# Moving one head's output weights onto eight DMA engines in small pieces, and splitting the result's transfer, in a decode kernel bound by its DMA stream

## The chip, the cores and the metric

One core of a Trainium2 chip. The metric is device microseconds of one execution. A "span" is what the profile covers, from the first to the last recorded instruction; it is about 1.8 us shorter than the time of the same execution (357.64 us and 355.8 us for the profiled execution of the kernel before).

## The reference

A decode step of one token through a conditioned transformer block, everything in bfloat16. It streams 149.4 MB, nearly all of it the key and value caches (8 heads of 32768 x 128, for each of K and V).

```python
def reference(A_x, A_k_cache, A_v_cache, A_wq, A_wo, B_x, B_w1, B_w2, c, w_mod):
    def _A_ref(x, k_cache, v_cache, wq, wo):          # 32 query heads, 8 kv heads, Dh = 128
        q = (x @ wq).reshape(B, Sq, Hq, Dh).transpose(0, 2, 1, 3)
        k, v = repeat(k_cache, 4), repeat(v_cache, 4)
        p = softmax(einsum('bhqd,bhkd->bhqk', q, k) * Dh ** -0.5)
        o = einsum('bhqk,bhkd->bhqd', p, v)
        return o.transpose(0, 2, 1, 3).reshape(B, Sq, Hq * Dh) @ wo      # wo is 4096 x 512
    def _B_ref(x, w1, w2):
        return maximum(x @ w1, 0) @ w2                                   # 512 -> 1792 -> 512
    sa, ca, ga, sb, cb, gb = split(silu(c) @ w_mod, 6)
    x = x + ga * _A_ref(layernorm(x) * (1 + ca) + sa, ...)
    return x + gb * _B_ref(layernorm(x) * (1 + cb) + sb, ...)
```

## The kernel before

Everything large comes through one ring of four slots of 32 KB a partition. All loads are issued on the sync engine's queue in one fixed order; a load goes out when the slot that it reuses is free.

```python
    WOP = [(0, Hkv // 2), (Hkv // 2, Hkv // 4), (3 * Hkv // 4, Hkv // 4)]   # wo in three parts, by kv heads
    ring = ctx.enter_context(tc.tile_pool(name="ring", bufs=4))
    ...
    def load(key):
        ...
        elif kind == "wo":
            t = ring.tile([P, WOP[key[1]][1] * REP, D], BF16, tag="slot", name="wo_sb")
            src = wo_v(key[1])
        ...
        stream_dma(t[:], src)                         # nc.sync.dma_start

    stream = [("wm",), ("wq",)] + [("k", 0, (2 * G, 2 * G + 1)) for G in range(NG)]
    for g in range(LAST):
        for G in range(NG):
            stream += [(kind, gg, (2 * G, 2 * G + 1)) for kind, gg in (("k", g + 1), ("v", g))]
    stream += [("v", LAST, (0, 1)), ("v", LAST, (2,)), ("wo", 0), ("wo", 1), ("v", LAST, (3,)), ("wo", 2)]
    stream += [("w1",)] + [("w2", i) for i in range(len(W2P))]
```

So the output weights of heads 0 to 5 are loaded near the end, and their products with the attention output run while the PE waits for the last piece of V (2.8 us of that wait are left in the profile). The tail after that piece is short: the product with the last part of wo, a layer norm, w1, w2, two vector operations and the result's transfer.

```python
                if g == LAST and u == NTILE - 1:
                    for i in range(len(WOP) - 1):
                        project(i)                    # 96 small matmuls, before the last V piece is used
                pv(g, u)
    ...
    project(len(WOP) - 1)
    ...
    nc.vector.tensor_tensor(out=o_bf[:], in0=o_rows[:], in1=x1_rows[:], op=ALU.add)
    nc.scalar.dma_start(
        out=out[0, 0].rearrange("(i n) -> i n", i=KT),
        in_=o_bf[:].rearrange("(i r) n -> i r n", r=32)[:, 0, :],
    )
```

## Time and profile before

| kernel before | us |
|---|---|
| first three runs, median (lowest to highest) | 357.16 (357.08 to 357.24) |
| with the fourth, profiled run | 357.2 (357.08 to 357.69) |
| the profiled execution, time and span | 357.64, 355.8 |

How to read it: the DMA engines are full from start to end (share 1.00 at 432 GB/s from 10 to 318 us, 0.58 in the last stretch, 347 to 352 us; in the packet records 16 packets are in flight at each of 17 moments from 10 to 330 us), so the time is bytes over rate plus the ragged end, at which the 16 engines do not finish together. The first fence is from the page of the kernel before (destination, source, issuing engine, count, KB each, us from issue to landing):

```profile
wo_sb<-in_A_wo_dram SPq DMA_DIRECT2D x1, 2048.0 KB
wo_sb<-in_A_wo_dram SPq DMA_DIRECT2D x2, 1024.0 KB, 10.2
```

The output weights, 4 MB, are three transfers, each over 128 partitions. The second is from the instructions in order of time (start us, duration us, engine, line, operation, and in brackets how long the engine had been idle and what ended that):

```profile
330.82 0.33 SPq L118 DMA_DIRECT2D Vsb<-in_A_v_cache_dram  x1
334.06 3.34 PE L461 MATMUL attnT_ps<-o_sb,wo_sb 128*128 128x1 bf16 x96
...
349.56 1.02 PE L525 MATMUL ffn_ps<-w_sb,hidT 128*1 128x128 bf16 x32 [0.98 <-DMA w_sb<-in_B_w_dram]
350.85 0.60 PE L525 MATMUL ffn_ps<-w_sb,hidT 128*1 128x128 bf16 x16 [0.26 <-DMA w_sb<-in_B_w_dram]
351.94 0.38 PE L525 MATMUL ffn_ps<-w_sb,hidT 128*1 128x128 bf16 x8 [0.50 <-DMA w_sb<-in_B_w_dram]
```

The last eight matmuls start at 351.94 us, after 0.50 us of idleness that a DMA of w2 ended. That start is the best single number for "when did the stream end".

### The profile page before, as it was taken

Reading aid. Unit: us, or ns where it says so; the run is one execution under the profiler, and the core shown is the slowest. Engines: PE = TensorE matmul, PEld = TensorE weight load, DVE = VectorE, ACT = ScalarE, POOL = GpSimd, SP = SyncE. Lnnn points to the kernel's source line nnn. Section 1 sums busy time; section 2 is a strip of 40 time slices with the busy share of each in tenths; the row PEclk is TensorE's granted clock in tenths of the full one; section 3 lists DMA queues with packets and bytes.
Section 4 is the critical chain, followed back from the end, with each engine's and each line's share of the span. In section 5 each row is a group of like instructions: output and inputs, shape, how many; then the busy total and the mean of one; then the engine's idle time right before and its main releaser. Section 6 shows DMA issues by size and latency. Waiting matters only on the chain.

```text
span 355.8 us, 4200 instructions
## 1 busy us (share of the span) xinstructions
PE 274.2 (77%) x1859; PEld 129.9 (37%) x1859; DVE 188.0 (53%) x210; ACT 30.8 (9%) x74; POOL 8.5 (2%) x14
## 2 busy tenths in 40 slices
PE   0552875998689885998499849987799859987754
PEld 0540322343333342443244324433243324335753
DVE  8414696783297409661759157642937184832020
ACT  1022002201200120001100120012000110003000
POOL 9000000000000000000000000000000000000000
PEclk9999968799969996999699978998599969997555
DMA  8999999999999999999999999999999999999993
GB/s 321 442 422 440 431 427 442 429 425 438 435 426 438 431 422 446 427 431 440 424 442 435 422 443 427 431 437 427 431 437 428 427 438 433 424 437 424 408 411 130
DMA packets 6604, 149.69 MB, mean 421 GB/s; under 512 B 697, under 2 KB 698, under 8 KB 1594
## 3 DMA queue, kind: packets, MB, share of 16 engines
q1 hardware_dynamic: 6578, 149.43, 97.9%
q8 instruction: 14, 0.23, 0.2%
q14 instruction: 4, 0.03, 0.0%
q10 hardware_dynamic: 8, 0.00, 0.0%
HBM read 149.42 MB, written 0.00 MB: 420 GB/s over the span
## 4 chain that ended last, share of the span: by engine, by line
DMA 47%; PE 34%; DVE 14%; issue 3%; ACT 0%; SPq 0%; DVEq 0%
DMA Ksb<-in_A_k_cache_dram 42%; PE S_ps L343 18%; PE o_ps L412 12%; DVE KTt L334 11%; DMA Vsb<-in_A_v_cache_dram 3%; DMA w_sb<-in_B_w_dram 2%; PE oT_ps L402 1%; DVE PT_g L381 1%; PE oT_ps L429 1%; DVE S_g L349 1%; PE L_ps L386 0%; SPq L118 0%; PE attnT_ps L461 0%; PE mT_ps L359 0%; ACT X L426 0%
## 5 line engine op out<-in xcount | busy, mean ns | idle before, releaser
L343 PE MATMUL S_ps<-KTt,qbd 128*128 128x512 bf16 x512 | 134.5, 423 | 29.8 <-DVE KTt L334 29.7
L334 DVE STREAM_TRANSPOSE KTt<-Ksb 128x2048 f32<-128x2048 f32 x64 | 142.6, 2279 | 21.1 <-DMA Ksb<-in_A_k_cache_dram 17.0
L412 PE MATMUL o_ps<-Vsb,PT_g 128*16 128x512 bf16 x448 | 99.0, 379 | 0.0
L343 PEld LDWEIGHTS <-qbd 128*128 128x128 bf16 x512 | 53.8, 106 | 104.6 <-issue 53.8
L412 PEld LDWEIGHTS <-PT_g 128*16 128x16 bf16 x448 | 39.1, 90 | 56.8 <-issue 3.0
L436 DVE TENSOR_TENSOR oT_sb<-oT_ps,Linv 128x4 bf16<-128x4 f32 x8 | 1.3, 162 | 71.8 <-PE oT_ps L429 57.3
L349 DVE TENSOR_SCALAR_CACHE_REDUCE S_g<-S_ps 128x512 f32<-128x512 f32 x16 | 11.1, 691 | 41.3 <-PE S_ps L343 41.3
L314 ACT COPY qbd<-qrep_sb 32x128 bf16<-32x128 bf16 x32 | 9.4, 295 | 160.0 <-PE S_ps L343 158.9
L386 PE MATMUL L_ps<-Lexp,ones_f 128*128 128x4 f32 x16 | 3.9, 314 | 13.0 <-DVE Lexp L384 13.0
L426 ACT COPY X<-o_ps 16x512 f32<-16x512 f32 x7 | 4.0, 574 | 110.4 <-PE o_ps L412 110.4
L402 PE MATMUL oT_ps<-PT_g,Vsb 128*128 128x4 bf16 x256 | 7.3, 166 | 4.4 <-DMA Vsb<-in_A_v_cache_dram 2.8
L381 DVE STREAM_TRANSPOSE PT_g<-P_g 128x1024 bf16<-128x1024 bf16 x8 | 9.9, 1232 | 0.0
L429 PE MATMUL oT_ps<-osel,X 16*128 16x4 f32 x56 | 7.3, 250 | 2.5 <-ACT nbias L373 2.5
L197 PE MATMUL xc_ps<-one,c_bd 8*128 8x1 bf16 x4 | 0.3, 172 | 11.6 <-DVE c_bd L187 11.6
L376 ACT ACTIVATE P_g<-S_g,nbias 128x1024 bf16<-128x1024 f32 x8 | 9.2, 1147 | 0.2
L402 PEld LDWEIGHTS <-Vsb 128*128 128x128 bf16 x256 | 7.2, 105 | 4.5 <-DMA Vsb<-in_A_v_cache_dram 2.9
L359 PE MATMUL mT_ps<-ident_f,m_p 128*1 128x128 f32 x8 | 2.2, 269 | 8.4 <-DVE m_p L357 8.4
L386 PEld LDWEIGHTS L_ps<-Lexp,ones_f 128*128 128x128 f32 x16 | 3.6, 271 | 13.5 <-issue 13.4
L155 DVE COPY sel<-ident_bf 128x128 bf16<-128x128 bf16 x4 | 7.8, 3823 | 0.4 <-POOL ident_bf masks.py:199 0.4
L429 PEld LDWEIGHTS oT_ps<-osel,X 16*128 16x128 f32 x56 | 6.7, 186 | 3.1 <-ACT nbias L373 3.1
L292 PE MATMUL qT_ps<-hT,wq_sb 128*128 128x1 bf16 x128 | 3.6, 165 | 3.2 <-DMA wq_sb<-in_A_wq_dram 3.2
L359 PEld LDWEIGHTS mT_ps<-ident_f,m_p 128*1 128x1 f32 x8 | 0.6, 80 | 12.2 <-issue 9.2
(94 smaller groups left out, 79.4 us busy)
## 6 DMA issues: line engine op xcount, KB each, us to landing
Ksb<-in_A_k_cache_dram SPq DMA_DIRECT2D x16, 4096.0 KB, 29.7
Vsb<-in_A_v_cache_dram SPq DMA_DIRECT2D x15, 4096.0 KB, 25.5
wq_sb<-in_A_wq_dram SPq DMA_DIRECT2D x1, 4096.0 KB, 19.7
Vsb<-in_A_v_cache_dram SPq DMA_DIRECT2D x2, 2048.0 KB, 15.5
wm_sb<-in_w_mod_dram SPq DMA_DIRECT2D x1, 3072.0 KB, 10.2
wo_sb<-in_A_wo_dram SPq DMA_DIRECT2D x1, 2048.0 KB
wo_sb<-in_A_wo_dram SPq DMA_DIRECT2D x2, 1024.0 KB, 10.2
w_sb<-in_B_w_dram SPq DMA_DIRECT2D x1, 1792.0 KB, 10.5
```

What stands on the lines that cost most here:

```text
L155: nc.vector.tensor_copy(out=sel[:, hp, :].rearrange("p (a c) -> p a c", a=4), in_=src)
L314: nc.scalar.copy(out=o, in_=i)
L334: nc.vector.transpose(out=KTt[:].bitcast(F32), in_=Ksb[:, 32 * half:32 * half + 32, :].rearrange("p j d -> p (j d)").bitcast(F32),)
L343: nc.tensor.matmul(S_ps[:], lhsT=qbd[g % 2][:, hp, s, :], rhs=KTv[:, 16 * sl:16 * sl + 16, h, :, par], start=(t4 == 0 and sl == 0 and hp = ...
L349: nc.vector.tensor_scalar(out=S_tiles[g][:, G, :], in0=S_ps[:], scalar1=1.0, scalar2=None, op0=ALU.mult, op1=ALU.max, accum_out=m_tiles[g] ...
L376: nc.scalar.activation(out=P_g[:], in_=S_g[:].rearrange("p g f -> p (g f)"), func=ACT.Exp, bias=nbias[:], scale=scale, accum_out=l_g[:],)
L381: nc.vector.transpose(out=PT_g[:], in_=P_g[:])
L386: nc.tensor.matmul(L_ps[:], lhsT=ones_f[:], rhs=Lexp[:], start=True, stop=True)
L402: nc.tensor.matmul(o_tiles[g][:], lhsT=Vsb[:, j, :], rhs=PT_g[:, c0:c0 + REP], start=(u == 0 and j == 0), stop=(u == NTILE - 1 and j == TK ...
L412: nc.tensor.matmul(o_tiles[g][:], lhsT=PT_g[:, c0:c0 + 16], rhs=Vsb.rearrange("p (s j) d -> p s j d", j=16)[:, :, j, :], start=(u == 0 and ...
L426: nc.scalar.copy(out=X[:], in_=oT_ps[:])
L429: nc.tensor.matmul(oT_ps[:], lhsT=X[:, s * Dh:(s + 1) * Dh], rhs=osel[:, s, :], start=(s == 0), stop=(s == 3),)
```

## The change

The weights of head 0 get a tile of their own on partitions 0 to 63. They are brought in by eight transfers of eight partitions each (64 KB), one after each K or V load in the turns of heads 1 and 2, in the first half of the stream. The weights of heads 1, 2 and 3 come in two transfers into one ring slot, ahead of the loads of head 4's turn, and heads 0 to 3 are projected in the middle of the stream instead of at the end. The weights of heads 4 to 7 stay late. The result leaves in two transfers of two rows, on the sync and the scalar queue. One buffer each of two smaller tiles was given up to make room. The intent, as I read it: to give eight of the sixteen DMA engines a little more and the other eight a little less, so that all end together, to take work from the end, and to save issuing time at the result.

```diff
-    WOP = [(0, Hkv // 2), (Hkv // 2, Hkv // 4), (3 * Hkv // 4, Hkv // 4)]
+    WOP = [(0, 1, P // 2), (1, 1, P), (2, 2, P), (4, 2, P), (6, 2, P)]      # third: partitions
...
+        if kind == "wo_lo":
+            lo = 32 * (key[1] // 4) + key[1] % 4
+            stream_dma(wo_lo[lo:lo + 29:4], wo_v(0)[lo:lo + 29:4])
+            loaded[key] = True
+            if key[1] == 7:
+                loaded[("wo", 0)] = wo_lo[:]
+            return
...
+        elif kind == "wo12":
+            n1, n2 = wo_rows(1), wo_rows(2)
+            t = ring.tile([P, n1 + n2, D], BF16, tag="slot", name="wo_sb")
+            loaded[("wo", 1)], loaded[("wo", 2)] = t[:, 0:n1, :], t[:, n1:n1 + n2, :]
+            stream_dma(loaded[("wo", 1)], wo_v(1))
+            stream_dma(loaded[("wo", 2)], wo_v(2))
+            return
...
     for g in range(LAST):
+        if g == Hkv // 2:
+            stream.append(("wo12",))
         for G in range(NG):
-            stream += [(kind, gg, (2 * G, 2 * G + 1)) for kind, gg in (("k", g + 1), ("v", g))]
-    stream += [("v", LAST, (0, 1)), ("v", LAST, (2,)), ("wo", 0), ("wo", 1), ("v", LAST, (3,)), ("wo", 2)]
+            for kind, gg in (("k", g + 1), ("v", g)):
+                stream.append((kind, gg, (2 * G, 2 * G + 1)))
+                if 1 <= g < 3:
+                    stream.append(("wo_lo", 4 * (g - 1) + 2 * G + (kind == "v")))
+    stream += [("v", LAST, (0, 1)), ("v", LAST, (2,)), ("wo", 3), ("v", LAST, (3,)), ("wo", 4)]
...
+    wo_lo = const.tile([P // 2, wo_rows(0), D], BF16)
...
-        PT_g = spool.tile([P, NG * 512], BF16, tag="PT_g", name="PT_g", bufs=3)
+        PT_g = spool.tile([P, NG * 512], BF16, tag="PT_g", name="PT_g")
...
-            X = spool.tile([16, 4 * Dh], F32, tag="X", name="X")
+            X = spool.tile([16, 4 * Dh], F32, tag="X", name="X", bufs=1)
...
     for g in range(Hkv):
+        if g == Hkv // 2:
+            for i in range(3):
+                project(i)
...
-                    for i in range(len(WOP) - 1):
-                        project(i)
+                    project(3)
...
-    nc.scalar.dma_start(out=out[0, 0].rearrange("(i n) -> i n", i=KT), in_=...)
+    o_v = o_bf[:].rearrange("(i r) n -> i r n", r=32)[:, 0, :]
+    out_v = out[0, 0].rearrange("(i n) -> i n", i=NROW)
+    nc.sync.dma_start(out=out_v[0:2], in_=o_v[0:2])
+    nc.scalar.dma_start(out=out_v[2:4], in_=o_v[2:4])
```

More of the change, by code (lines that the diff above doesn't have):

```diff
@@ L45 @@
     NG = NTILE // 2
-    WOP = [(0, Hkv // 2), (Hkv // 2, Hkv // 4), (3 * Hkv // 4, Hkv // 4)]
+    WOP = [(0, 1, P // 2), (1, 1, P), (2, 2, P), (4, 2, P), (6, 2, P)]
     LAST = Hkv - 1
+    NROW = 4
+    RW = D // NROW
     FB = 2
@@ L63, in wo_v, with wo_rows @@
     def wo_v(i):
-        g0, n = WOP[i]
-        return A_wo[g0 * REP * Dh:(g0 + n) * REP * Dh, :].rearrange("(p r) d -> p r d", p=P)
+        g0, n, pp = WOP[i]
+        return A_wo[g0 * REP * Dh:(g0 + n) * REP * Dh, :].rearrange("(p r) d -> p r d", p=pp)
+    def wo_rows(i):
+        return WOP[i][1] * REP * Dh // WOP[i][2]
     w1_v = B_w1.rearrange("(p kt) f -> p kt f", p=P)
@@ L100, in load @@
         elif kind == "wo":
-            t = ring.tile([P, WOP[key[1]][1] * REP, D], BF16, tag="slot", name="wo_sb")
+            t = ring.tile([P, wo_rows(key[1]), D], BF16, tag="slot", name="wo_sb")
             src = wo_v(key[1])
+        elif kind == "wo12":
[5 more added lines that the diff above has]
+            return
         elif kind == "w1":
@@ L165 @@
     cmask, rsel = {}, {}
-    for n in sorted({n * REP for _, n in WOP}):
+    for n in sorted({wo_rows(i) for i in range(len(WOP))}):
         cmask[n] = const.tile([P, P // n], F32, name=f"cmask{n}")
@@ L180 @@
     oT_sb = const.tile([P, Hq], BF16)
-    oA = [const.tile([P, n * REP, P // (n * REP)], BF16, name=f"oA{i}") for i, (_, n) in enumerate(WOP)]
+    oA = [const.tile([P, n * REP, P // wo_rows(i)], BF16, name=f"oA{i}") for i, (_, n, _) in enumerate(WOP)]
     one8 = const.tile([8, 1], BF16)
@@ L255, with to_rows @@
     nc.vector.tensor_copy(out=modT_sb[:], in_=modT_ps[:])
-    def rows4(src_T, r_ps, name):
-        for i in range(KT):
+    def to_rows(src_T, r_ps, name):
+        for i in range(NROW):
             dst = r_ps[32 * i:32 * i + 1, :].rearrange("o (n kt) -> o kt n", kt=KT)
@@ L262, in rows4 @@
                 m = nc.tensor.matmul(
-                    dst[:, kt, :], lhsT=src_T[:, kt:kt + 1], rhs=ident_f[:, 32 * i:32 * i + 32],
+                    dst[:, kt, :], lhsT=src_T[:, kt:kt + 1], rhs=ident_f[:, RW // KT * i:RW // KT * (i + 1)],
                     start=True, stop=True, skip_group_check=True,
@@ L266, in rows4 @@
                 tc.stamp_issue_order_token(m.ins, "pe_tail")
-        r_sb = const.tile([P, P], F32, name=f"{name}_sb")
+        r_sb = const.tile([32 * NROW, RW], F32, name=f"{name}_sb")
         nc.scalar.copy(out=r_sb[:], in_=r_ps)
         return r_sb
-    gb_ps = ps_s.tile([P, 512], F32, tag="s", name="gb_ps")[:, 0:P]
+    gb_ps = ps_s.tile([P, 512], F32, tag="s", name="gb_ps")[0:32 * NROW, 0:RW]
     nc.vector.memset(gb_ps, 0.0)
-    gb_rows = rows4(modT_sb[:, 5 * KT:6 * KT], gb_ps, "gb_rows")
+    gb_rows = to_rows(modT_sb[:, 5 * KT:6 * KT], gb_ps, "gb_rows")
     hT = const.tile([P, KT], BF16)
@@ L418, in part_of @@
     def part_of(g):
-        return [i for i, (g0, n) in enumerate(WOP) if g0 <= g < g0 + n][0]
+        return [i for i, (g0, n, _) in enumerate(WOP) if g0 <= g < g0 + n][0]
     def normalise(g):
@@ L432, in normalise @@
         i = part_of(g)
-        g0, n = WOP[i]
-        CH = P // (n * REP)
+        g0 = WOP[i][0]
+        RH = wo_rows(i)
+        CH = Dh // RH
         o_g = oT_sb[:, REP * g:REP * (g + 1)]
@@ L439, in normalise @@
             in0=o_g.unsqueeze(2).to_broadcast([P, REP, CH]),
-            in1=cmask[n * REP][:].unsqueeze(1).to_broadcast([P, REP, CH]), op=ALU.mult,
+            in1=cmask[RH][:].unsqueeze(1).to_broadcast([P, REP, CH]), op=ALU.mult,
         )
@@ L445, in spread @@
     def spread(i):
-        n = WOP[i][1] * REP
-        o2_ps = small_ps([P, n], "o2_ps")
+        pp, RH = WOP[i][2], wo_rows(i)
+        o2_ps = small_ps([pp, RH], "o2_ps")
         nc.tensor.matmul(
-            o2_ps[:], lhsT=oA[i][:].rearrange("p h c -> p (h c)"), rhs=rsel[n][:], start=True, stop=True,
+            o2_ps[:], lhsT=oA[i][:].rearrange("p h c -> p (h c)"), rhs=rsel[RH][:], start=True, stop=True,
         )
-        o2 = const.tile([P, n], BF16, name=f"o2_sb{i}")
+        o2 = const.tile([pp, RH], BF16, name=f"o2_sb{i}")
         nc.vector.tensor_copy(out=o2[:], in_=o2_ps[:])
@@ L456, in project @@
     def project(i):
-        n = WOP[i][1] * REP
         wo_sb = need(("wo", i))
-        for r in range(n):
+        for r in range(wo_rows(i)):
             for ko in range(KT):
@@ L463, in project @@
                     lhsT=wo_sb[:, r, :].rearrange("p (m ko) -> p ko m", ko=KT)[:, ko, :],
-                    rhs=o2_tiles[i][:, r:r + 1], start=False, stop=(i == len(WOP) - 1 and r == n - 1),
-                    skip_group_check=True,
+                    rhs=o2_tiles[i][:, r:r + 1], start=False,
+                    stop=(i == len(WOP) - 1 and r == wo_rows(i) - 1), skip_group_check=True,
                 )
@@ L487 @@
         normalise(g)
-        if g + 1 == sum(WOP[part_of(g)]):
+        if g + 1 == sum(WOP[part_of(g)][:2]):
             spread(part_of(g))
     project(len(WOP) - 1)
-    ffn_ps = ps_s.tile([P, 512], F32, tag="s", name="ffn_ps")[:, 0:P]
+    ffn_ps = ps_s.tile([P, 512], F32, tag="s", name="ffn_ps")[0:32 * NROW, 0:RW]
     nc.vector.memset(ffn_ps, 0.0)
-    x1_ps = ps_s.tile([P, 512], F32, tag="s", name="x1_ps")[:, 0:P]
+    x1_ps = ps_s.tile([P, 512], F32, tag="s", name="x1_ps")[0:32 * NROW, 0:RW]
     nc.vector.memset(x1_ps, 0.0)
@@ L504 @@
     layernorm_T(x1T[:], stat2, h2T[:], modT_sb[:, 3 * KT:4 * KT], ncb[:], "ln2")
-    x1_rows = rows4(x1T[:], x1_ps, "x1_rows")
+    x1_rows = to_rows(x1T[:], x1_ps, "x1_rows")
     w1_sb = need(("w1",))
@@ L523 @@
                 ft = (base + a) * FB + b
-                for i in range(KT):
+                for i in range(NROW):
                     nc.tensor.matmul(
                         ffn_ps[32 * i:32 * i + 1, :], lhsT=hidT[:, ft:ft + 1],
-                        rhs=w2_sb[:, a, b, i * P:(i + 1) * P], start=False, stop=(ft == FT - 1),
+                        rhs=w2_sb[:, a, b, i * RW:(i + 1) * RW], start=False, stop=(ft == FT - 1),
                         skip_group_check=True,
                     )
-    o_rows = const.tile([P, P], F32)
+    o_rows = const.tile([32 * NROW, RW], F32)
     nc.vector.tensor_tensor(out=o_rows[:], in0=ffn_ps, in1=gb_rows[:], op=ALU.mult)
-    o_bf = const.tile([P, P], BF16)
+    o_bf = const.tile([32 * NROW, RW], BF16)
     nc.vector.tensor_tensor(out=o_bf[:], in0=o_rows[:], in1=x1_rows[:], op=ALU.add)
-    nc.scalar.dma_start(
-        out=out[0, 0].rearrange("(i n) -> i n", i=KT),
-        in_=o_bf[:].rearrange("(i r) n -> i r n", r=32)[:, 0, :],
-    )
+    o_v = o_bf[:].rearrange("(i r) n -> i r n", r=32)[:, 0, :]
+    out_v = out[0, 0].rearrange("(i n) -> i n", i=NROW)
+    nc.sync.dma_start(out=out_v[0:2], in_=o_v[0:2])
+    nc.scalar.dma_start(out=out_v[2:4], in_=o_v[2:4])
 _INS = ['A_x', 'A_k_cache', 'A_v_cache', 'A_wq', 'A_wo', 'B_x', 'B_w1', 'B_w2', 'c', 'w_mod']
```

## The prediction

> **What bounds the kernel now.** I read the page's summary first, then the stretches of time by engine, the DMA queue's own waits, the chain in order of time at the end, and last the DMA packet records one by one.
>
> ```profile
> PE 274.2 (77%) x1859; PEld 129.9 (37%) x1859; DVE 188.0 (53%) x210; ACT 30.8 (9%) x74; POOL 8.5 (2%) x14
> DMA  8999999999999999999999999999999999999993
> q1 hardware_dynamic: 6578, 149.43, 97.9%
> q8 instruction: 14, 0.23, 0.2%
> ```
>
> No compute engine is full, and the 16 DMA engines are busy in all slices but the last. The stretches (columns: length, five engines, clock, DMA share, GB/s) give the rate:
>
> ```profile
> 10.00:318.00 308.00, 250.03 (x1293) 110.19 (x1294) 174.77 (x181) 25.62 (x65) 0.00 (x0) 0.91 1.00 432
> 318.00:340.00 22.00, 15.61 (x325) 12.14 (x322) 1.83 (x5) 3.16 (x5) 0.00 (x0) 0.67 0.98 413
> 340.00:347.00 7.00, 4.99 (x133) 4.64 (x134) 2.02 (x14) 0.56 (x2) 0.00 (x0) 0.50 1.00 412
> 347.00:352.00 5.00, 3.26 (x108) 2.86 (x112) 0.00 (x0) 0.18 (x1) 0.00 (x0) 0.50 0.58 221
> ```
>
> From 10 to 318 us the DMA share is 1.00 at 432 GB/s, so the time is bytes over rate: 149.43 MB / 432 GB/s = 345.9 us, plus a head (first packet at 1.76 us) and a tail. The long DMA pieces of the chain are queueing, not latency: a 4096 KB transfer takes 4.19 MB / 432 GB/s = 9.7 us, yet lands 29.7 us after issue:
>
> ```profile
> Ksb<-in_A_k_cache_dram SPq DMA_DIRECT2D x16, 4096.0 KB, 29.7
> SPq L118 <- DVE KTt L334: 136.7, 15, 15.0
> SPq L118 <- PE Mb_ps L371: 72.7, 7, 11.1
> ```
>
> About 20 us of other work is still queued when the issuer, which waits for ring slots, gets one. That is the slack which compute may use before a DMA engine runs dry. The end:
>
> ```profile
> 340.22 1.88 PE oT_ps L402 x64
> 343.04 1.21 PE attnT_ps L461 x32
> 344.27 7.63 DMA w_sb<-in_B_w_dram
> 351.94 0.41 PE ffn_ps L525 x7
> 352.38 0.30 DVE o_rows L531
> 352.77 0.29 DVE o_bf L533
> 353.10 1.10 ACTq L534 DMA_DIRECT2D out_dram<-o_bf  x1
> ```
>
> The last piece of w2 lands at 351.90 us; eight matmuls, two vector operations and the result's transfer follow (last line from the instructions in order of time). The 347 to 352 row has only 58% DMA share: the 16 engines don't finish together. That row decides this case.
>
> The packet records tell them apart. A 32 KB packet takes 1213 ns on its engine (27 GB/s), each starting as the one before on that engine ends, so engines can be followed by phase. The 8-row load of c puts a 128-byte packet on eight of them; I call those low, the rest high. Lag of each engine near 318 us, against an engine moving the same bytes at 27.09 GB/s from the span's start: low 2.58, 2.67, 2.90, 2.93, 3.60, 4.18, 4.39, 4.62; high 3.32, 3.36, 4.09, 4.17, 4.20, 4.91, 5.64, 5.89. The differences are mostly the 16 KB instruction packets of q8: each delays its engine 1.4 us. They recur with period 8 over eight engines: six high, two low. Between 318 us and the end four more come (331.1, 337.4, 343.8, 349.8 us), by the sequence all on high engines. The sixteen completions of the last w2 piece fit: ten engines at 349.07 to 350.13, six at 350.95, 351.07, 351.09, 351.20, 351.44 and 351.90. Lag plus 345.5 gives the slow ones (5.89: 351.4).
>
> [...]
>
> **The change part by part.**
>
> Head 0 of wo, 512 KB: before, it was part of a 128-partition load, 32 KB per engine. Now eight transfers of 8 x 8 KB give each low engine 64 KB and high engines none. At 27.09 GB/s, 32 KB is 1.21 us: low engines +1.21, high -1.21. I add 0.1 us to low for eight more completions. This lies on the path that sets the end, and I take it as the purpose.
>
> Ends. High before: lags 4.09, 4.17, 4.20 with a late fetch of 1.4 become about 5.5 to 5.6; 5.64 and 5.89 stay; 4.91 with the fetch at 349.8 is the 351.90. After: 351.90 - 1.21 = 350.7 at most. Low after: the worst, 4.62, lands at 4.62 + 345.5 + 1.21 + 0.1 = 351.4; the next (4.39) at 351.2. So the end moves from 351.90 to about 351.4: -0.5 us. Only the excess over the new slowest engine is gained, not 1.21.
>
> The last V piece (2 MB): issue moves earlier. Before, it waited for a ring slot until 330.82 us, and the fastest engines idled up to 0.7 us. Now it takes the slot freed one place earlier. The slowest engines had no gap, so nothing on the path. Its landing at 340.17 is set by the slowest engine too: about +0.05. Then the compute between it and the first w2 matmul (349.56, of which 0.7 us after the hidden layer was spent waiting for w2) stays just covered.
>
> Projection: 64 wo matmuls left the tail and 80 stand at heads 2 to 4. In the tail 96 took 3.34 us (35 ns each), ending at 337.4 us while PE then waited for V until 340.22: hidden before. In the middle 80 x 35 ns = 2.8 us on PE, against some 20 us of slack: hidden. PE gains 36 rows in all, DVE two, both under the stream.
>
> Ring: a 1.5 MB buffer takes one of four slots that otherwise hold 4 MB, so for one turn 2.7 MB or 6.2 us less is queued ahead: 20 - 6 is still over 10. PT and X lose one buffer each; both are released a whole head before reuse (about 38 us between heads), so no wait.
>
> Result: two transfers of two rows instead of one of four. The 1.10 us issue on the scalar engine's queue remains; the sync queue's usual 0.33 us fits beside it. I take 0 to -0.2, say -0.05.
>
> Sum: -0.5 + 0.05 - 0.05 = -0.5 us; 357.16 becomes 356.7.
>
> **The rivals.** (1) No balance gain: the extra 1.21 us makes a low engine the last, or an extra 8 KB fetch (0.85 us each; the four in the stream all sat on low engines) falls on a loaded one.[...] For: the predicted low end, 351.4, is only 0.5 under the present end. Result 357.1 to 357.5. (2) Full gain: later fetches shift to other engines and every engine ends within a microsecond; the mean finish is then the bound, 356.0.[...] (3) The smaller ring slot or the matmuls in the middle starve the DMA engines: each microsecond of idleness costs one, 358 to 360. Against: the slack above. (4) The removed 0.7 us gap mattered: 356.3; against it, only the early engines have it.
>
> **Range and chances.** The mechanism is worth 0 to 1.2 us, the result's split 0.2, and runs spread 0.16 us (357.08 to 357.24). So 356.0 to 357.4. Two per cent is 7.1 us, beyond every rival: within 2% 0.98, faster 0.01, slower 0.01.
>
> **What would show it.** The same 432 GB/s in the middle; the last w2 landing near 351.4 with its completions closer together, and now low engines last; the last V piece issued some 7 us earlier yet landing near 340; attention projections at heads 2 to 4 without new DMA gaps. It would be wrong if the small transfers spread over all 16 engines, if the DMA share dips below 1.00 between 160 and 320 us, or if the end of w2 does not move while the time does.

The sum has all its terms: -0.5 for the end of the stream, +0.05 for the last V piece, -0.05 for the result, so 357.16 becomes 356.7. But its first term rests on two things that the trace before does not show. That each transfer of eight partitions would go to the same eight engines was an assumption; that trace has only the load of c, eight packets of 128 bytes at 9.7 to 10.3 us. (The trace of the changed kernel bears it out, see below.) And the 0.1 us for eight completions is an estimate: the 4-byte packets of the load queue take 9 ns each in that trace (676 of 681), so eight take 0.07 us.

## The result, and the profile after

| | median us (lowest to highest), runs | ratio to before, 95% |
|---|---|---|
| before | 357.2 (357.08 to 357.69), 4 | |
| changed | 359.01 (358.33 to 359.63), 4 | 1.0048 (1.0026 to 1.0070) |

Ratios here are the mean time of one kernel's fast runs over that of the other's of the same rounds, so not quite the ratio of the medians. The sign is wrong: 0.5% slower where I had 0.1% faster, and outside my range, which ended at 357.4. The profile of the changed kernel is of its 358.33 us execution, with a span of 356.5 us. From its page:

```profile
PE 276.8 (78%) x1877; PEld 130.8 (37%) x1877; DVE 188.7 (53%) x212; ACT 31.0 (9%) x74; POOL 8.5 (2%) x14
...
DMA  8999999999999999999999999999999999999992
...
q1 hardware_dynamic: 6854, 149.43, 97.8%
q8 instruction: 14, 0.23, 0.2%
...
Ksb<-in_A_k_cache_dram SPq DMA_DIRECT2D x16, 4096.0 KB, 29.3
```

The engines' work grew by the few rows expected. The DMA queue is as full and as deep as before (29.3 us from issue to landing, 29.7 before). The same stretches as in the prediction (from:to, length, busy us of PE, PEld, DVE, ACT, POOL, clock, DMA share, GB/s):

```profile
10.00:318.00 308.00, 251.26 (x1359) 112.00 (x1360) 173.94 (x177) 25.86 (x65) 0.00 (x0) 0.91 1.00 432
318.00:340.00 22.00, 16.97 (x277) 11.24 (x275) 3.35 (x11) 3.16 (x5) 0.00 (x0) 0.82 0.98 415
340.00:347.00 7.00, 4.92 (x131) 4.54 (x131) 2.03 (x14) 0.56 (x2) 0.00 (x0) 0.50 1.00 410
347.00:352.00 5.00, 2.77 (x96) 2.57 (x100) 0.00 (x0) 0.18 (x1) 0.00 (x0) 0.50 0.60 229
```

From 10 to 318 us the rate is 432 GB/s at a share of 1.00, exactly as before: the smaller ring slot and the 80 projections in the middle starved nothing, and PE did its 66 extra matmuls there without the stream waiting. The last stretch even moved 8 GB/s more. But work was left for after 352 us. The chain that ended last (start us, us, what) shows where:

```profile
327.95 12.31 DMA Vsb<-in_A_v_cache_dram
...
340.31 1.88 PE oT_ps L430 x64
...
342.21 9.66 DMA w_sb<-in_B_w_dram
...
351.91 0.59 PE ffn_ps L555 x16
...
352.53 0.41 PE ffn_ps L555 x8
...
352.96 0.30 DVE o_rows L561
...
353.36 0.29 DVE o_bf L563
```

Up to the last V piece it is the same chain: PE gets it at 340.31 us instead of 340.22. Then the last eight matmuls with w2 start at 352.53 instead of 351.94 us, 0.59 us later, and everything behind them follows. The instructions in order of time say what came in late:

```profile
327.95 0.33 SPq L140 DMA_DIRECT2D Vsb<-in_A_v_cache_dram  x1
...
349.59 1.02 PE L555 MATMUL ffn_ps<-w_sb,hidT 128*1 128x128 bf16 x32 [0.87 <-DMA w_sb<-in_B_w_dram]
351.91 1.01 PE L555 MATMUL ffn_ps<-w_sb,hidT 128*1 128x128 bf16 x24 [1.30 <-DMA w_sb<-in_B_w_dram]
...
353.68 0.57 SPq L566 DMA_DIRECT2D out_dram<-o_bf  x1
353.68 1.41 ACTq L567 DMA_DIRECT2D out_dram<-o_bf  x1
```

The first piece of w2 was there as before (349.59 against 349.56), but the second came 1.06 us later (351.91 against 350.85): PE sat 1.30 us waiting for it. And the result's issue on the scalar queue takes 1.41 us, where the single one took 1.10.

The DMA view of the stretch from 348 to 351 us has one line more to read (queue, kind: packets, MB, share):

```profile
q8 instruction: 1, 0.02, 1.8%
```

One 16 KB fetch of instructions fell into the last three microseconds, as it did in the kernel before. Which of the 16 engines it falls on this view does not say. For that I followed the packet records: each engine starts its next packet when its last ends (within 4 ns in this trace), so 16 chains can be told apart by their phase.

In this trace the engine that ended last, at 352.05 us, was a low one, one of the eight that carry the small transfers. (Of the sixteen completions of the last w2 piece thirteen come by 350.72 us, then 351.25, 351.46 and, alone, 352.49.) Fetches at 167.3 and 189.5 us had fallen on two low engines, and in a cycle of eight the one at 348.9 us is due on the first of these again; the fetches' own durations, shown further down, say the same. By my reading of the trace before, all late fetches should have fallen on high engines.

### The profile page after: what moved, and what is told of

The parts are those of the page before. It is cut to its first block, busy times and chain, and to the rows that moved or that the text cites. A ratio compares the mean times of both kernels' runs of the same rounds, so it can differ in the third digit from the quotient of the medians.

```text
span 356.5 us, 4248 instructions
## 1 busy us (share of the span) xinstructions
PE 276.8 (78%) x1877; PEld 130.8 (37%) x1877; DVE 188.7 (53%) x212; ACT 31.0 (9%) x74; POOL 8.5 (2%) x14
## 4 chain that ended last, share of the span: by engine, by line
DMA 46%; PE 33%; DVE 16%; issue 3%; SPq 0%; ACT 0%; DVEq 0%
DMA Ksb<-in_A_k_cache_dram 40%; PE S_ps L371 17%; PE o_ps L440 14%; DVE KTt L362 13%; DMA Vsb<-in_A_v_cache_dram 3%; DMA w_sb<-in_B_w_dram 3%; DVE S_g L377 1%; DVE PT_g L409 1%; PE oT_ps L457 1%; PE oT_ps L430 1%; PE mT_ps L387 0%; SPq L140 0%; PE ffn_ps L555 0%; PE L_ps L414 0%; DVE m_p L385 0%
## 5 line engine op out<-in xcount | busy, mean ns | idle before, releaser
L440 PE MATMUL o_ps<-Vsb,PT_g 128*16 128x512 bf16 x448 | 100.7, 384 | 0.0
L416 DVE RECIPROCAL Linv<-L_ps 128x4 f32<-128x4 f32 x8 | 1.4, 176 | 13.8 <-PE L_ps L414 12.7
L489 PE MATMUL attnT_ps<-o_sb,wo_sb 128*128 128x1 bf16 x112 | 4.4, 172 | 2.2 <-issue 1.7
## 6 DMA issues: line engine op xcount, KB each, us to landing
Ksb<-in_A_k_cache_dram SPq DMA_DIRECT2D x16, 4096.0 KB, 29.3
```

What stands on the lines that cost most here:

```text
L440: nc.tensor.matmul(o_tiles[g][:], lhsT=PT_g[:, c0:c0 + 16], rhs=Vsb.rearrange("p (s j) d -> p s j d", j=16)[:, :, j, :], start=(u == 0 and ...
L489: nc.tensor.matmul(attnT_ps[:, ko:ko + 1], lhsT=wo_sb[:, r, :].rearrange("p (m ko) -> p ko m", ko=KT)[:, ko, :], rhs=o2_tiles[i][:, r:r + ...
```

## The experiments

The letters in the expectations are only my working names for the theories; the figures beside them say what each forecast. The theories in words: that the extra data on the low engines sets the end; that the split result costs time; that the rest of the change (ring slot, projections in the middle, late issues) costs time; and, from the third group of runs on, that the place at which the sequence of instruction fetches falls decides from execution to execution.

The first four kernels ran on one chip in five rounds, where the kernel before took 357.29 us (356.82 to 357.81, 11 runs); the next four on another, with 357.35 us (357.2 to 357.83, 11 runs).

**The changed kernel again, unedited.**

> The changed kernel unedited, for a second trace and more times. In the first trace the last w2 piece landed at 352.49 us (before: 351.90) and a low engine was last, delayed 1.4 us by an instruction packet at 348.9 us. Theory A (the small transfers overload the low engines, and which engines the instruction packets fall on changes from run to run): times 1.0 to 2.5 us over before with a wider spread than before has, and in the new trace again a low engine last, at 352 to 354 us. Theory B (the split result costs the time): w2 lands at about 351.9 and the tail after it is longer. Theory C (the work moved to the middle starves the DMA engines): a DMA share under 1.00 between 160 and 320 us.

Measured: 358.38 us (356.99 to 358.75, 6 runs), 1.0024 of before (1.0010 to 1.0038). The slowdown is real, but half of the first figure, and one run of the six took 356.99 us, 1.28 us less than the next. Spans of the six: 356.6, 355.2, 356.6, 356.7, 356.6, 356.5. That is not noise around one value, but two values. The chain of the profiled run (358.39 us) ends like the first one:

```profile
343.23 8.67 DMA w_sb<-in_B_w_dram
...
351.94 0.60 PE ffn_ps L555 x16
...
352.57 0.41 PE ffn_ps L555 x8
```

**The result in one transfer again, the rest as changed.**

```diff
-    nc.sync.dma_start(out=out_v[0:2], in_=o_v[0:2])
-    nc.scalar.dma_start(out=out_v[2:4], in_=o_v[2:4])
+    nc.scalar.dma_start(out=out_v, in_=o_v)
```

> The changed kernel with the result in one transfer on the scalar engine's queue, as before. Theory B: most of the 1.7 us comes back, 357.3 to 357.7. Theory A: only what the issue shows, 1.41 us against 1.10, comes back, that is 0.2 to 0.4 us: about 358.6.

Measured: 358.69 us (356.82 to 358.81, 6 runs), 1.0028 (1.0012 to 1.0045). Undoing the split did not bring the time back. The profiled run was the odd one, 356.82 us, with a span of 355.0; the other five took 358.41 to 358.81. Its chain:

```profile
341.98 8.61 DMA w_sb<-in_B_w_dram
...
350.63 0.59 PE ffn_ps L555 x15
...
351.26 0.41 PE ffn_ps L555 x8
```

The last eight matmuls start at 351.26 us: 1.3 us before the two slow traces, and 0.68 us before the kernel before. The same stream of transfers can thus end as early as I had predicted. Its result is issued in one piece of 1.11 us:

```profile
352.41 1.11 ACTq L566 DMA_DIRECT2D out_dram<-o_bf  x1
```

**Head 0's weights over all 16 engines, in one transfer, the rest as changed.**

```diff
-    WOP = [(0, 1, P // 2), (1, 1, P), (2, 2, P), (4, 2, P), (6, 2, P)]
+    WOP = [(0, 1, P), (1, 1, P), (2, 2, P), (4, 2, P), (6, 2, P)]
-            lo = 32 * (key[1] // 4) + key[1] % 4
-            stream_dma(wo_lo[lo:lo + 29:4], wo_v(0)[lo:lo + 29:4])
+            stream_dma(wo_lo[:], wo_v(0))
-                if 1 <= g < 3:
+                if g == 1 and G == 0 and kind == "k":
-    wo_lo = const.tile([P // 2, wo_rows(0), D], BF16)
+    wo_lo = const.tile([P, wo_rows(0), D], BF16)
```

> The changed kernel with wo of head 0 on 128 partitions in one transfer over all 16 engines, at the place of the first small one; the rest as changed, the split result too. Theory A: the low engines lose 1.31 us, the high ones gain 1.21 us; if the low ones were last, 0.7 to 1.3 us comes back, 357.5 to 358.3. Theory B or C: nothing, 359.

Measured: 357.41 us (357.16 to 357.6, 5 runs), 1.0001 (0.9989 to 1.0013). With the same bytes spread evenly (and in one transfer instead of eight), 0.97 us of the 1.09 us between the changed kernel and before on this chip are gone, and so are the two values: the five spans lie between 355.4 and 355.7. The last eight matmuls are back near their old place:

```profile
342.54 8.64 DMA w_sb<-in_B_w_dram
...
351.23 0.60 PE ffn_ps L553 x16
...
351.83 0.41 PE ffn_ps L553 x8
```

So the loss sits in the small transfers to eight engines.

**The kernel before with the result split, nothing else.** The edit puts rows 0 and 1 on the sync queue, 2 and 3 on the scalar queue, as in the change.

> The kernel before with nothing but the result split into two rows on each of two queues. Theory B: 358.5 to 359. Theory A: 0.2 to 0.4 us over before, from the scalar queue's longer issue. My own prediction on record: -0.05 us.

Measured: 357.67 us (357.58 to 357.94, 5 runs), 1.0010 (0.9997 to 1.0023). The interval holds zero, so the time alone is not conclusive. The tail is more telling: from the end of the last vector operation to the end of the span it takes 2.89 us, with one transfer 2.70. In five traces with a split result that tail was 2.78 to 2.90 us, in five with one transfer 2.59 to 2.71: about 0.2 us more. In order of time:

```profile
353.03 0.60 SPq L536 DMA_DIRECT2D out_dram<-o_bf  x1
353.03 1.34 ACTq L537 DMA_DIRECT2D out_dram<-o_bf  x1
```

Issued side by side, the scalar engine's transfer of two rows took longer to issue (1.34 us) than its transfer of four rows did alone (1.10). The sync engine's own is done in 0.60 us, but the end waits for the later of the two.

**Half of head 0's extra on the low engines.**

```diff
-            stream_dma(wo_lo[lo:lo + 29:4], wo_v(0)[lo:lo + 29:4])
+            stream_dma(wo_lo[lo:lo + 29:4, 0:4, :], wo_v(0)[lo:lo + 29:4, 0:4, :])
+            if key[1] == 0:
+                stream_dma(wo_lo[:, 4:8, :], wo_v(0)[:, 4:8, :])
```

> The changed kernel with half the dose: the eight small transfers carry 4 KB instead of 8 KB per partition, the other half of head 0's wo comes in one 64-partition transfer[...]; split result kept.[...] Theory A (low engines last): half way between the version with 16 engines (357.41) and the changed one (358.38), so 357.7 to 358.0. Theory D (each small transfer costs something by itself, whatever its size): as the changed kernel, 358.4.

Measured: 359.74 us (358.62 to 360.52, 6 runs), 1.0062 (1.0048 to 1.0075). This fits neither forecast; half the change is worse than the whole. It is a faulty experiment. The second transfer was meant to run over all 16 engines, which no figure here shows, but it writes only 64 partitions. The stretches of the profiled run (columns as above) show what that did:

```profile
80.00:87.00 7.00, 5.93 (x29) 2.45 (x27) 3.49 (x6) 1.18 (x4) 0.00 (x0) 1.00 1.01 435
87.00:91.00 4.00, 4.00 (x20) 1.63 (x19) 0.00 (x0) 0.00 (x0) 0.00 (x0) 1.00 1.20 298
91.00:160.00 69.00, 58.35 (x254) 25.08 (x253) 42.00 (x37) 5.04 (x12) 0.00 (x0) 0.90 0.99 427
```

For 4 us packets overlap so that the share is 1.20, and yet 298 GB/s are moved instead of 435: 4 KB packets took up to 474 ns instead of 159, 32 KB packets up to 2507 instead of 1213. By the bytes moved, the stream is 2.2 us behind that of the changed kernel from 100 us to 300 us. The size of the packets is not the reason: the run with head 0's weights over 16 engines loads them at the same place in 4 KB packets too, but to 128 partitions, and there each took 159 ns and the stream fell behind by nothing. What makes the 64-partition load slower was not shown. The run says nothing on the question it was built for. It only suggests why the change brings these rows in eight small loads, rather than in one plain 64-partition load.

**Head 0 over 16 engines and the result in one transfer.** What remains of the change is the ring slot of heads 1 to 3, the projections in the middle and the earlier issues.

> Head 0's wo over 16 engines and the result in one transfer: what remains of the change is the ring buffer for heads 1 to 3, the projections in the middle, and the earlier issue of the last V piece. The split alone cost 0.38 us on the kernel before, so 356.9 to 357.2 and 0.1 to 0.4 us under before if these costs add (theory A); equal to before (357.3) if the split costs nothing here.

Measured: 357.75 us (357.34 to 357.97, 5 runs), 1.0008 (0.9995 to 1.0021). The rest of the change is worth nothing, or a few tenths to the bad; the interval holds zero. The forecast of 0.1 to 0.4 us under before missed, and the other one, equal to before, fits: the times don't show here what the tail shows of the split (2.78 us with it in the run with head 0's weights over 16 engines, 2.59 in this one).

**The kernel before with 512 KB more, on the low engines only.** Eight loads of 64 KB into an unused tile, at the places and in the shape of the change's; the result is right.

```diff
+    def dummy(j):
+        lo = 32 * (j // 4) + j % 4
+        src = A_wo[0:512, :].rearrange("(p r) d -> p r d", p=P // 2)
+        stream_dma(scratch[lo:lo + 29:4], src[lo:lo + 29:4])
+                if 1 <= g < 3:
+                    stream.append(("dummy", 4 * (g - 1) + 2 * G + (kind == "v")))
+    scratch = const.tile([P // 2, 8, D], BF16)
```

(and the two smaller tiles with a buffer less, as in the change, to make room)

> The kernel before with eight additional 8-partition transfers of 64 KB into a scratch buffer, at the same places in the stream, read by nobody (one buffer less of PT and X makes room, as in the change). 512 KB more, all on the low engines: 2.42 us more of data on each, and 0.1 for eight completions; high engines unchanged. Theory A: low engines trail high ones by little in most runs, so 1.7 to 2.5 us over before, more than the same bytes spread over all engines cost. My prediction on record had the low engines 1.3 us ahead of the last: 1.2 us over before.

Measured: 359.45 us (359.44 to 360.15), 1.0061 (1.0049 to 1.0073): 2.1 us more than before. In order of time:

```profile
351.91 1.02 PE L537 MATMUL ffn_ps<-w_sb,hidT 128*1 128x128 bf16 x32 [0.78 <-DMA w_sb<-in_B_w_dram]
353.18 1.02 PE L537 MATMUL ffn_ps<-w_sb,hidT 128*1 128x128 bf16 x24 [0.25 <-DMA w_sb<-in_B_w_dram]
```

64 KB on each low engine is 2.43 us by the prediction's 27 GB/s, plus 0.1 for the completions: 2.5 us. Of that 2.1 show. So the low engines of the kernel before, as they fell in this execution, were only some 0.4 us from being the last. The prediction had 351.90 - (4.62 + 345.5) = 1.8 us between the slowest low engine and the end. (The expectation misquotes it as 1.3; the prediction's own figures give 0.7 us over before, not 1.2.) In this trace two low engines were hit by two fetches each, at 62.1 and 332.2, and at 90.2 and 338.4 us; in the profiled execution of the kernel before each was hit once. A fetch of 1.4 us is the difference between 1.8 and 0.4. (The 1.4 from the records of the kernel before, first ten fetches: the fetch's packet takes 879 to 962 ns, and the 32 KB packet behind it 1681 to 1764 ns instead of 1213.)

**The same 512 KB over all 16 engines.** One load of 128 partitions at the place of the first of the eight.

> The same 512 KB into a scratch buffer in one 128-partition transfer over 16 engines: 1.21 us more of data on each engine. All theories: 1.2 us over before (1.0 to 1.4). It is the measure for the run on the low engines.

Measured: 358.63 us (358.27 to 359.0), 1.0036 (1.0024 to 1.0047): 1.28 us more, where 32 KB per engine are 1.21. In order of time:

```profile
350.71 1.02 PE L535 MATMUL ffn_ps<-w_sb,hidT 128*1 128x128 bf16 x32 [0.89 <-DMA w_sb<-in_B_w_dram]
...
352.98 0.38 PE L535 MATMUL ffn_ps<-w_sb,hidT 128*1 128x128 bf16 x8 [0.34 <-DMA w_sb<-in_B_w_dram]
```

Bytes spread evenly cost what they cost: 1.04 us between 351.94 and 352.98. On the low engines alone the same bytes cost 0.8 us more.

**Seven looks at the changed kernel, unedited.** By now I had traces of the changed kernel that ended at 352.5 us and one (with one result transfer) at 351.26, and had a theory for it. The 14 instruction fetches of an execution go round a cycle of eight engines, six high and two low, and in the changed kernel's traces the two low ones are neighbours in that cycle (the fetches' durations, shown below, say so). Fourteen is eight and six: the first six places of the cycle are hit twice, the seventh and eighth once. If the cycle always began at the same place, that would be a property of the kernel. If it begins somewhere else in each execution, the low engines are sometimes the seventh and eighth, and spared, and sometimes not. The theory says: low engines in places 7 and 8, fast; anywhere else, slow. Looks, each with its own trace, test it.

> The changed kernel unedited, one look for the instruction packets. Their period-8 sequence over six high and two adjacent low engines starts at another place in each execution; 14 packets give six engines two and two engines one. Theory A: about 357 us only if both low engines of the sequence get one packet each (the seventh and eighth place, one start in eight), else 358.2 to 359.6. A slow run with one packet on each low engine, or a fast one with two on either, would refute it.

> A further look at the changed kernel, with the same expectation: 358.2 to 359.6 us if a low engine takes two instruction packets, about 357 us if neither does.

> A further look at the changed kernel, with the same expectation: 358.2 to 359.6 us if a low engine takes two instruction packets, about 357 us if neither does.

> A look at the changed kernel for one more start of the instruction packets' sequence. Theory A: span about 355.3 us if neither low engine of the sequence takes two packets, 356.5 us and more if one does; the slowest group (357.5 us and more) should show a low engine that takes two 16 KB packets and an 8 KB one besides. Another grouping would refute it.

> As the look before it: span about 355.3 us if neither low engine of the sequence takes two instruction packets, 356.5 us or more if one does.

> One more look, same expectation: span about 355.3 us if neither low engine of the sequence takes two instruction packets, 356.5 us or more if one does.

> One more look, same expectation: span about 355.3 us if neither low engine of the sequence takes two instruction packets, 356.5 us or more if one does.

Here are the ten traces that carry head 0's weights on the low engines. The place is that of the first low engine in the cycle; the times are those of the fetches that hit low engines; "stream end" is the end of the last w2 packet in the records.

| trace | place | fetches on low engines, us | stream end | last eight matmuls | span | time |
|---|---|---|---|---|---|---|
| changed, first | 6 | 167.3, 348.9; 189.5 | 352.05 | 352.53 | 356.5 | 358.33 |
| changed again | 3 | 63.0, 321.1; 92.4, 336.9 | 352.20 | 352.57 | 356.6 | 358.39 |
| one result transfer | 7 | 187.7; 215.9 | 350.91 | 351.26 | 355.0 | 356.82 |
| look 1 | 7 | 189.3; 215.9 | 350.91 | 351.28 | 355.3 | 357.08 |
| look 2 | 6 | 166.1, 349.4; 187.9 | 352.09 | 352.58 | 356.6 | 359.94 |
| look 3 | 7 | 189.3; 216.0 | 350.99 | 351.33 | 355.3 | 357.13 |
| look 4 | 7 | 187.9; 216.0 | 350.95 | 351.33 | 355.3 | 357.27 |
| look 5 | 6 | 165.9, 349.0; 187.8 | 351.94 | 352.43 | 356.4 | 358.22 |
| look 6 | 7 | 187.8; 216.0 | 350.94 | 351.32 | 355.3 | 357.12 |
| look 7 | 7 | 187.7; 215.8 | 350.78 | 351.16 | 355.2 | 356.96 |

In place 6 the low engine that was hit sixth, at about 166 us, is due again as fourteenth, at about 349 us. Six traces in place 7 have spans of 355.0 to 355.3 us; four in place 6 or 3 have 356.4 to 356.6; there is no exception. A caution: two engines that come into the same phase can be confused in the records, above all after 340 us. The early fetches are read directly (in look 3 only one of the two low ones is; the other is inferred); that the one at 349 us falls on the low engine hit sixth is inferred from the cycle. In look 2 it can be seen as well: that engine's last w2 packets took 2.04 us, where those of its undisturbed neighbours took 0.64, a difference of 1.4.

The records hold a second mark of the engine, which needs no phase: how long the fetch's own packet took.

```text
ns of the 14 fetch packets of an execution in order, eight to a row
changed, first   933 928 961 967 949 879 886 942
                 932 922 962 960 951 879
changed again    962 955 886 881 938 933 928 961
                 961 947 886 886 935 931
look 1           936 938 921 962 964 954 886 879
                 935 931 924 961 961 948
```

Each value comes back eight fetches later within 8 ns, so the cycle of eight can be read directly. In all 17 traces two neighbours of the cycle take 878 to 888 ns and every other fetch 921 or more; where the phase is clear (167.3 and 189.5 us in the first trace) the short ones are those on low engines. In the ten traces of the table the short ones stand at exactly the times listed, those near 349 us (879, 887 and 881 ns) and the second one of look 3 included. In the kernel before they are the fetches at 203.5 and 234.2 us, which is place 7.

A control stands in the kept traces too. With head 0's weights spread evenly, one trace has place 2 (short fetches at 28.0, 63.2, 288.5 and 324.9 us) and its stream ends at 351.50 us; with the result in one transfer besides, the trace has place 7 and ends at 351.60; the kernel before, in place 7, ends at 351.47. Without the extra bytes on the low engines the place does not show; with them it is worth about 1.0 to 1.4 us (351.94 to 352.20 against 350.78 to 350.99).

The order of the times itself needs no such reading: of the 17 executions of the changed kernel, six have spans of 355.2 to 355.3 us, eight 356.4 to 356.7, three 357.0 to 357.7, and none lies between 355.3 and 356.4.

The instructions of look 1 in order of time, to be held against those of the first trace of the changed kernel, which is the same program:

```profile
349.36 1.02 PE L555 MATMUL ffn_ps<-w_sb,hidT 128*1 128x128 bf16 x32 [0.89 <-DMA w_sb<-in_B_w_dram]
350.65 1.01 PE L555 MATMUL ffn_ps<-w_sb,hidT 128*1 128x128 bf16 x24 [0.27 <-DMA w_sb<-in_B_w_dram]
```

The first piece comes 0.2 us sooner, the second at 350.65 instead of 351.91 us.

The sizes close too. Take the low engines of the kernel before in the two cases:

```text
place 7: lag 4.62 (the prediction's figure) + 345.5 + 1.21 (32 KB) + 0.1 (completions) = 351.4 predicted
         (345.5 was fitted to landings, 0.3 to 0.4 us behind the last packet)
         measured last landing of the five unedited looks in place 7: 351.12 to 351.29, 0.1 to 0.3 sooner
place 3: the kernel before with 64 KB more per low engine had place 3; its last packet ended at 353.43
         353.43 - 2.5 = 350.9 for the low engines without them (an estimate)
         350.9 + 1.3 = 352.2 for the changed kernel; measured in its trace with place 3: 352.20
```

## Why the prediction was wrong, point by point

**What bounds the kernel**, the stream and the moment when its slowest engine ends, was right: in every trace the chain to the last eight matmuls goes through a wait for w2, and the differences between the kernels' spans lie there and in the result's transfer.

**Low engines +1.21 us, high -1.21.** Right in size. In look 1, which is in the case that the prediction saw, thirteen of the sixteen completions are in by 350.31 us (ten by 350.13 in the trace before, the other six from 350.94 to 351.90), and the last three come at 351.12, 351.22 and 351.24; the prediction's three largest low lags (4.18, 4.39, 4.62), with 1.21 and 0.1 added, give 350.99, 351.20 and 351.43. The eight completions cost about 0.05 us by the phases at 66 and 163 us, half of what was assumed. (That each of the eight-row transfers used eight engines is read from the trace of the changed kernel, where each shows as eight 8 KB packets that start within 0.91 us, on eight chains; that it was the same eight each time, from the offsets between the eight starts, which are the same within 1 ns in all eight transfers, 87.27 to 158.12 us, and from the phases of those chains, which between 66 and 163 us shift by what 64 KB ask, within 4 ns in seven of the eight.)

**"By the sequence all on high engines": the step that failed.** The prediction took the cycle seen in one trace, with the two low engines in places 7 and 8, for a property of the kernel. It is one of several ways in which an execution can fall. In the case that I saw, the prediction holds for the sign and for the end of the stream: in look 1 the last eight matmuls start 0.66 us sooner than in the profiled execution before (0.5 predicted), and the split result gives about 0.2 back. The gain in time is smaller, because that profiled execution (span 355.8 us) lay above the median of its kernel: the looks in place 7 have spans of 355.2 to 355.3 us against medians of 355.5 and 355.6 us in the two sets of repeated runs, a gain of 0.2 to 0.4. In the other cases a low engine gets a second fetch of 1.4 us, and the span becomes 356.4 to 356.6, a loss of 0.8 to 1.1. That accounts for the first of the four runs of the result (358.33 us); the other three lie up to 1.3 us beyond it, which stays open. "Lag 4.62" for the worst low engine was a number of one execution, and the loaded low engines have nothing to spare. The trace shown to me was the case that favours the change. (In the kernel before, all engines move as many packets, so its chains are harder to tell apart; that its trace is in place 7 rests on the short packets. Its times, 356.82 to 357.83 us in the 22 runs of the two chips, have one value, as one expects if without extra bytes it does not matter which engines are hit.)

**Rival 2** expected that later fetches shift to other engines. What the traces show: there are 14 fetches in both kernels. The times of the fetches hardly move from trace to trace of the changed kernel (less than 3 us at any of the fourteen; the first is at 19.4 to 19.8 us, the last at 348.5 to 349.8 us in the traces of the two kernels). The engines on which they fall do.

**Rival 1** named the right event, an extra fetch on a loaded low engine, but took it for an 8 KB one (in the trace before, the first three of the stream's four take 309 ns each, and the 32 KB packet behind them 1461 to 1751 ns instead of 1213: 0.56 to 0.85 us), and gave it 357.1 to 357.5 us. It was one of the 16 KB ones, and the slow runs take 358.2 to 358.8. (Three of the first four took up to 359.63, see below.) I gave it too little room because I treated one profile as the distribution.

**"The result: 0 to -0.2, say -0.05"**: wrong in sign. The split costs about 0.2 us of tail. The "1.10 us issue on the scalar engine's queue remains" failed: it became 1.34 to 1.41 us, and the sync queue's "usual 0.33 us" became 0.56 to 0.61. So the split saved no issuing time.

**The last V piece "issued some 7 us earlier"**: it was 2.87 us (327.95 against 330.82); the effect, nothing on the path, was right (it landed 0.10 us later, 340.27 against 340.17).

**Rivals 3 and 4** fell: no gap in the stream between 160 and 320 us, and the rest of the change by itself is 1.0008 (0.9995 to 1.0021) of before. The projection moved as foreseen. By tile, head 0's weights (line, engine, operation, count: shortest, median, longest ns, first and last start):

```profile
L489 PE MATMUL attnT_ps<-o_sb,wo_lo x32: 167/168/190, 169.8 to 170.8; 64*128 64x1 bf16 x32
L140 SPq DMA_DIRECT2D wo_lo<-in_A_wo_dram x8: 647/647/776, 66.8 to 132.9; - x8
```

Thirty-two products, all at about 170 us, hidden.

**A slip in its working** that changes nothing: the gap of "up to 0.7 us" before the last V piece is, in the packet records, one or two engines without a packet for some 0.2 us around 332 us, so rival 4 had even less to gain.

**The sum as it came out** on the first chip of the experiments: about +1.0 us for the small transfers in the slow placement (358.38 against 357.41 with the bytes spread), about +0.2 for the split result, and the rest within the noise: 358.4 against 357.3.

**Still open.** The first four runs of the changed kernel took 358.33, 359.63, 358.76 and 359.27 us; spans of 357.0 to 357.7 as in three of them never recurred with a trace, so what was worse there is unknown. Look 2 has a normal slow span of 356.6 us but 3.3 us outside it instead of 1.8, with an instruction packet at 358.84 us; unexplained. The slow runs of the kernel with one result transfer (358.41 to 358.81) are not faster than those of the changed kernel, though their tail should be 0.2 us shorter. What decides where the cycle starts I don't know. In the 17 traces the place is 7 in ten, 6 in three, 3 in two and 2 in two, so the "one start in eight" of the first look's expectation is not borne out. The fast kind came in none of the first four runs of the changed kernel, in one of six repeated ones, and in five of seven looks; these were not all on one chip, and whether the chip matters was not tested. In the run with 64 KB more on the low engines only, place 7 should give a span of about 356.5 us by the same sum (4.62 + 345.5 + 2.43 + 0.1 = 352.65, and 3.9 us from landing to the end, an estimate from its trace); its five spans are 357.6 to 358.4, so either none of them fell there or the sum is not the whole. That the place is the cause, rather than a companion of it, rests on the ten traces, on the removal of the small transfers, which took the two values away, and on the evenly loaded trace in place 2, which is not slow; no run could set the starting place on purpose. No version measured beats both kernels; the even spread of head 0's weights (1.0001) equals the kernel before.

## What to carry to other kernels

In this kernel, bound by its DMA stream (share 1.00 at 432 GB/s), the slowest of the engines set the end, and the change, which shifts 1.21 us of bytes between engines, gained 0.2 to 0.4 us in one placement of the disturbances (spans of 355.2 to 355.3 us) and lost 0.8 to 1.1 in the others (356.4 to 356.6). Before such a shift elsewhere, ask whether the *worst* placement, not the observed one, still lets the receiving engines finish before the givers did. One profile shows one placement: before tuning a balance to a microsecond, take several traces of the same program and look whether the spans have one value or two. And split a tiny last transfer over two queues only after measuring it; here the slower of two issues took longer (1.34 to 1.41 us) than the single one (1.10).
